# A gated attention and MLP kernel: the last w4 products as fp32r parts at the MLP's end, the second key tile's scores before them, and small weight copies on POOL

## The chip, the cores and the metric

The kernel runs on one core of a Trainium2 chip. A core has five engines with instruction streams of their own: TensorE (PE, matrix products; "PEld" is its weight load), VectorE (DVE), ScalarE (ACT, activations), GpSimd (POOL) and SyncE (SP, which here issues most DMAs). They work on a 128-partition on-chip memory (SBUF) and, for matrix results, on eight PSUM banks of 128 x 512 fp32 elements. Engines wait for each other only by semaphores, and an engine carries out its instructions in the order in which they stand. The metric is device time in microseconds (us). The kernel before takes 912.61 us (median of three runs, 912.49 to 913.4).

## The reference

One input x of 2048 tokens by 448 features goes through two branches. Branch A is attention with 16 query heads of 28 elements that share one key and one value head. Branch B is a shifted token mix and an MLP. A sigmoid gate per token mixes them.

```python
def _A_ref(x, wq, wk, wv, wo):
    q = (x @ wq).reshape(B, S, H, Dh).transpose(0, 2, 1, 3)
    k = x @ wk
    v = x @ wv
    scores = jnp.einsum("bhqd,bkd->bhqk", q, k) * (Dh ** -0.5)
    p = _softmax(scores, axis=-1)
    o = jnp.einsum("bhqk,bkd->bhqd", p, v)
    return o.transpose(0, 2, 1, 3).reshape(B, S, H * Dh) @ wo

def _B_ref(x, w1, w2, w3, w4):
    h = _gelu(_layernorm(x) @ w1)
    ...
    x1 = x + hs
    h2 = _gelu(_layernorm(x1) @ w3) @ w4
    return x1 + h2

g = sigmoid((x * gate_w).sum(-1))
return g * a + (1 - g) * b
```

Here B = 1, S = 2048, D = 448, H = 16, F = 1792 (the width between w3 and w4).

## The kernel before

Three stages follow each other. Stage 1 (to about 125 us) makes queries, keys and values and the token mix, and leaves x1 in SBUF. Stage 2 is the MLP, in four blocks `b` of 512 tokens. Stage 3 is attention, from about 400 us to the end, in 16 units `u`: 512 queries of four heads against all keys.

**Numbers in two parts.** Large products are made with fp32r operands split in a high and a low part (`...h`, `...l`), three products for one: high by high, low by high, high by low. A weight's parts come from `split_w` (w3) and `split_w4` (w4): ACT writes the high part, DVE subtracts to get the low one, and POOL clears a spare corner. The fourth chunk of w3 is only 64 rows deep, so its other 64 rows hold a copy of the raw weight in the low part; `split_w_high` makes it at L114, on ACT.

**The MLP.** In each block `w3_part(b, f)` makes the 14 pieces `f` of 128 hidden features: eleven products into a `mm` bank `g` (L136 to L140), then two activations (`gh` at L688, `gf` at L689) and DVE's difference `gl` (L690). Two pieces later `w4_part` adds the piece's share of w4: for each of four token tiles `t` three 128x448 products into `acc[t]` (L698 to L700). DVE adds `acc` to x1 at L764. While block 0 runs, the weights of pieces to come are split. The last piece of the last block is an exception: it gets one activation in plain fp32 (`gf_late`, L683), its weights come by a DMA of their own (`w4_late`, L740), and its products are left to attention.

**Attention.** A key tile is 128 keys. Its scores (L205) are 12 products of 32 rows each, four heads side by side, into four banks; exponentials (L258) follow on ACT; the products of exponentials and values (`values`, L892) come a round later. A round `c` handles tiles 2c and 2c+1 of the running unit. Eight banks are shared: four `singles` (bank_0 to bank_3), which the MLP knows as its `mm`, `misc` and `mx` banks, and two `pairs` of two banks, which take over the MLP's four `acc` banks. In a full round the first tile's last two heads are copied to SBUF by DVE (L953) so that their pair is free early, and ACT reads that copy last; everything else ACT reads from PSUM. Values results land in two of the singles, DVE adds them into `o` (L813, L817).

**Jobs.** A round can carry a "job" on PE behind its values products: a 128x224 product in column quarters (L843) and one DVE addition. Jobs are the output products of the unit before (eight a unit, from round 12 on) and, in the first rounds, the eight halves of the last w4 piece: three in round 0 (`JOBS_0`), one each in rounds 3, 5, 7, 9 and 11 (`IDLE` and `MAX_AT` leave out the others). Rounds 2 and 10 carry small products for the next unit's maxima (L212) instead; these need its queries, which SP loads (L190) after POOL has cleared `qr` (L783), and which DVE casts (L194).

**The seam.** The order of all instructions is the order of the code. At the end of the MLP stand the scores of key tile 0 (into the singles), then the products of the last but one w4 piece, then round 0.

Of the kernel before, what the change touches and what calls it, by code (L numbers as in the profile page):

```python
# [17 lines left out]
P = 128  # L18
S = 2048
D = 448  # L20
# [22 lines left out]
def gated_mix_kernel(  # L43
# [63 lines left out]
            nc.vector.tensor_tensor(wl[0:64, 3, cols], raw[0:64, 3, cols], f32(wh)[0:64, 3, cols], ALU.subtract)  # L107
            nc.scalar.copy(wl[64:128, 3, cols], raw[64:128, 3, cols])

    def split_w_high(raw, wh, wl):  # L110
        nc.scalar.copy(wh[:, 0:3, :], raw[:, 0:3, :])
        nc.gpsimd.memset(f32(wh)[64:128, 3, :], 0.0)
        nc.scalar.copy(wh[0:64, 3, :], raw[0:64, 3, :])
        nc.scalar.copy(wl[64:128, 3, :], raw[64:128, 3, :])  # L114
# [6 lines left out]
    def split_w(raw, wh, wl):  # L121
        split_w_high(raw, wh, wl)
        split_w_low(raw, wh, wl)

    def split_a(raw, ah, al, c0, c1, high=True):
# [131 lines left out]
    def exps(p, heads, source=None):  # L257
        nc.scalar.activation(p[:, heads], p[:, heads] if source is None else source, AF.Exp, scale=SCALE)  # L258
# [4 lines left out]
    with tc.tile_pool(name="s1b", bufs=1) as s1b, \  # L263
# [325 lines left out]
        kh_of.append(late.tile([P, S], F32R, name="kh"))  # L589
        qh0 = late.tile([P, 512], F32R, name="qh0")  # L590
        ql0 = late.tile([P, 512], F32R, name="ql0")
        gf_late = late.tile([P, 512], F32, name="gf_late")
        w4_late = late.tile([P, D], F32, name="w4_late")
        bigs = ctx.enter_context(tc.tile_pool(name="bigs", bufs=1, side="right", reuse_waits="tile"))
        s2a = ctx2.enter_context(tc.tile_pool(name="s2a", bufs=1, side="right", reuse_waits="tile"))
        w3h, w3l, w4h, w4l = [], [], [], []
# [3 lines left out]
        def big(name):  # L600
            return bigs.tile([P, 2048], F32, tag="big", bufs=2, name=name)
# [10 lines left out]
            nc.sync.dma_start(raw4[i], w4[i * 256:i * 256 + 256, :].rearrange("(c p) n -> p c n", p=P))  # L612

        def split_w3(i):
            split_w(raw3[i], w3h[i], w3l[i])

        def split_w4(i):
            nc.scalar.copy(w4h[i], raw4[i])
# [47 lines left out]
    with tc.tile_pool(name="s2", bufs=1, reuse_waits="tile") as s2, \  # L666
# [11 lines left out]
        def w3_part(b, f):  # L678
            i, k = divmod(f, 2)
            ps = mm_tile(f"g_{b}_{f}")  # L680
            proj(ps, w3h[i][:, :, k * P:(k + 1) * P], w3l[i][:, :, k * P:(k + 1) * P], *acts[b])
            if (b, f) == (NB - 1, NF - 1):
                nc.scalar.activation(gf_late, ps, AF.Gelu_apprx_tanh)  # L683
                return None
            gh = s2.tile([P, 512], F32R, tag="gh", bufs=3, name=f"gh_{b}_{f}")
            gl = s2.tile([P, 512], F32R, tag="gl", bufs=3, name=f"gl_{b}_{f}")
            gf = s2.tile([P, 512], F32, tag="gf", bufs=1, name=f"gf_{b}_{f}")
            nc.scalar.activation(gh, ps, AF.Gelu_apprx_tanh)  # L688
            nc.scalar.activation(gf, ps, AF.Gelu_apprx_tanh)  # L689
            nc.vector.tensor_sub(gl, gf, f32(gh))  # L690
            return gh, gl

        def w4_part(f, t, g, acc, stop=NF - 1):
# [4 lines left out]
            nc.tensor.matmul(ps, gh[:, tok], w4h[i][:, k, :], start=(f == 0), stop=False)  # L698
            nc.tensor.matmul(ps, gh[:, tok], w4l[i][:, k, :], start=False, stop=False)  # L699
            nc.tensor.matmul(ps, gl[:, tok], w4h[i][:, k, :], start=False, stop=(f == stop))  # L700

        for b in range(NB):
            acc = [ps2.tile([P, 512], F32, tag="acc", bufs=4, name=f"acc_{b}_{t}") for t in range(4)]
            gs = {}
            for f in range(NF):
                if f == 9 and b + 1 < NB:
                    mv, rs = layernorm_stats(s2a, b + 1)
                if f == 10 and b + 1 < NB:
                    xt4 = big(f"xt4_{b + 1}")[:, 0:4 * D].rearrange("p (f t j) -> p f t j", f=NE, t=4)
                if f in (10, 11) and b + 1 < NB:  # L710
                    for t in (2 * f - 20, 2 * f - 19):
                        xn = s2a.tile([P, 512], F32, tag="xn", bufs=1, name=f"xn_{b + 1}_{t}")[:, 0:D]
# [12 lines left out]
                if b == 1 and f == 0:  # L725
                    nc.gpsimd.tensor_tensor(gg, invE, gz, ALU.pow)
                    nc.vector.tensor_scalar(gg, gg, 1.0, None, op0=ALU.add)
                    nc.vector.reciprocal(gg, gg)
                    nc.vector.tensor_scalar(gi, gg, -1.0, 1.0, op0=ALU.mult, op1=ALU.add)
                if b == NB - 1 and f == 4:  # L730
                    weigh_x1(0, 4 * b)
                if b == 1 and f == 1:
                    nc.gpsimd.memset(khd, 0.0)
                    for j in range(4):
                        h = slice(32 * j, 32 * j + DH)
                        nc.gpsimd.tensor_copy(khd[h, j * MK:(j + 1) * MK], f32(kh_of[0])[h, 0:MK])
                    qr0 = s2a.tile([P, 512], F32, tag="xn", bufs=1, name="qr_0")
                    nc.gpsimd.memset(qr0, 0.0)
                    q_load(0, qr0)
                    nc.sync.dma_start(w4_late, w4[F - P:F, :])  # L740
                if b == 1 and f == 5:
                    q_high(0, qh0, ql0)
                    q_low(0)
                if f >= 2:
                    for t in range(4):
                        w4_part(f - 2, t, gs[f - 2], acc)
                        if b > 1 and t % 2 == 0 and f < NF - 1:
                            fill()
            if b == NB - 1:
                singles = [mm_tile("bank_0"), mm_tile("bank_1"), misc_tile("bank_2"), max_tile("bank_3")]  # L750
                scores(0, 0, singles)
                nc.scalar.activation(first, powt, AF.Exp)
                p_first = big("p_0_0").rearrange("p (j n) -> p j n", j=4)
                for j in range(4):
                    exps(p_first, slice(j, j + 1), singles[j].unsqueeze(1))
            for t in range(4):
                w4_part(NF - 2, t, gs[NF - 2], acc, NF - 2 if b == NB - 1 else NF - 1)
                if b + 1 < NB:
                    ln_split(b + 1, t, t + 1)
            for t in range(4):  # L760
                if b < NB - 1:
                    w4_part(NF - 1, t, gs[NF - 1], acc)
                xt = x1[:, 4 * b + t, :]
                nc.vector.tensor_add(xt, xt, acc[t][:, 0:D])  # L764
        assert not fills
# [3 lines left out]
    with tc.tile_pool(name="s3", bufs=1, reuse_waits="tile") as s3, \  # L769
# [100 lines left out]

        weigh_x1(NT - 4, NT)

        def w4_products(t, ps, cols):
            by_columns(ps, gf_late, t, w4_late[:, cols])

        def w4_add(t, ps, cols):
            n = NT - 4 + t
            nc.vector.scalar_tensor_tensor(x1[:, n, cols], ps, gi[:, n:n + 1], x1[:, n, cols],
                                           op0=ALU.mult, op1=ALU.add)

        p_of = {0: p_first}

        def score_tiles(u, kt, first, second, third, fourth):
            scores(u, kt, [first, second, third, fourth])
# [9 lines left out]
                if qs.stop == 512:  # L894
                    p_of.pop(k)

        jobs = [(w4_products, w4_add, (t,), cols) for t in range(4) for cols in halves]
        left, right, both, front = slice(0, 1), slice(1, 2), slice(2, 4), slice(0, 2)
        sums, norms, later = [], [], []
        pv = None  # L900
        MAX_AT = 2
# [14 lines left out]
        def run_jobs(ps, n):  # L916
            job_adds(job_products(ps, n))

        NC = NU * NT // 2
        JOBS_0 = (2, 1)  # L920
        IDLE = range(2, 12, 2)
        HINTS = {8 * NT // 2 + 4: [mybir.EngineType.SP],
                 14 * NT // 2 - 2: [mybir.EngineType.DVE, mybir.EngineType.Activation]}
        for c in range(NC):
# [1 line left out]
            k = 2 * c  # L926
            s0, s1, s2, s3_ = singles if c % 2 == 0 else singles[2:] + singles[:2]
            if c == 0:
                pb = score_tiles(u, 1, s2, s3_, s0, s1)
                for j, ps in enumerate((s2, s3_, s0, s1)):  # L930
                    exps(pb, slice(j, j + 1), ps.unsqueeze(1))
                pa = score_tiles(u, 2, *(q[:, h] for q in pairs for h in range(2)))
                nc.vector.tensor_copy(pa[:, front], pairs[0])
                for ps, n in zip((s2, s3_), JOBS_0):
                    run_jobs(ps, n)
                exps(pa, both, pairs[1])
                exps(pa, front)
                pairs.reverse()
                continue
            if c > 1:  # L940
# [43 lines left out]
            elif i == MAX_AT:  # L984
                run_jobs(pairs[0][:, 0], 1)
            values((k - 2, k - 1), s1[:, q0], q1)
            adds = job_products(s0[:, q1], 0 if c in IDLE or c == 1 else 1)
            values_end(v, s1[:, q0], q1)
            job_adds(adds)
            if i == 0 and v < NU - 1:  # L990
# [153 lines left out]
```

## Time and profile before

| what | value |
|---|---|
| median of three runs | 912.61 us (912.49 to 913.4) |
| the profiled execution | 912.95 us |
| its span, from first to last instruction | 911.2 us |
| TensorE clock granted, in tenths, all slices | 9 (9 is 90% or more) |
| ACT busy, 400 to 911 us | 496.67 us of 511 |
| PE busy, 400 to 911 us | 505.70 us of 511 |
| w4 jobs in attention (L843, w_late) | 64 matmul records, 353 ns each |
| w4 products of one piece in the MLP (L698 to L700) | 12 matmuls, about 365 ns each, overlapping |

A row of the timeline reads: start in us, duration, engine, line, operation, output <- inputs, shape, count of instructions merged, and in brackets how long the engine sat idle before and who released it. Matmuls overlap in the array, so the time that one adds is read from start to start. ACT's rows overlap too; what an exponential adds is the distance to the next start. In the page each digit is the busy share of one of 40 slices. A row of the windows gives a stretch of time, its length, and the busy time and instructions of PE, PEld, DVE, ACT and POOL.

### The profile page before, as it was taken

The numbers are of one execution on the slowest core, as the hardware profiler recorded it, in microseconds if no ns is written. First come the engines' busy times: TensorE is split into PE (matmuls) and PEld (weight loads), VectorE is DVE, ScalarE is ACT, GpSimd is POOL, SyncE is SP. The second block draws the span as 40 slices with busy tenths as digits, with TensorE's granted clock in tenths as the row PEclk, the third lists the DMA queues.
The fourth block names the chain that finished last, engine by engine and source line by source line (L and its number), as shares of the span: only waits on it lengthen the run. The fifth ranks groups of instructions, "written<-read, shape, count | busy, mean of one in ns | idle before, by whom it ended". The sixth has DMA issues, their size and how long they took to land.

```text
span 911.2 us, 24150 instructions
## 1 busy us (share of the span) xinstructions
PE 904.7 (99%) x10360; PEld 627.6 (69%) x10360; DVE 517.1 (57%) x961; ACT 633.1 (69%) x1003; POOL 78.3 (9%) x116
## 2 busy tenths in 40 slices
PE   9999999999999999999999999999999999999998
PEld 6788888888888888875555555555555555555554
DVE  4665273631431531136766776776767667767665
ACT  5442344332131231269999999999999999999995
POOL 3243330200000520020000000000000000000000
PEclk9999999999999999999999999999999999999999
DMA  8832654120110020010000001000011000010001
GB/s 306 282 97 54 150 168 131 32 75 1 35 53 2 18 69 1 1 52 24 14 25 14 24 15 55 23 25 17 24 33 36 25 14 25 15 55 13 15 14 44
DMA packets 40582, 47.31 MB, mean 52 GB/s; under 512 B 10136, under 2 KB 28632, under 8 KB 40472
## 3 DMA queue, kind: packets, MB, share of 16 engines
q1 hardware_dynamic: 37304, 40.30, 15.1%
q10 hardware_dynamic: 3168, 5.44, 1.6%
q8 instruction: 82, 1.34, 0.6%
q14 instruction: 28, 0.23, 0.1%
HBM read 32.56 MB, written 11.67 MB: 49 GB/s over the span
## 4 chain that ended last, share of the span: by engine, by line
PE 98%; ACT 2%; DVE 0%; issue 0%
PE bank L892 26%; PE bank L205 19%; PE bank L843 6%; PE acc L700 5%; PE acc L698 5%; PE acc L699 5%; PE g L137 4%; PE g L138 4%; PE g L136 4%; PE pair L205 3%; ACT p L258 2%; PE hs L474 1%; PE hs L475 1%; PE g L139 1%; PE g L140 1%; PE h L137 1%
## 5 line engine op out<-in xcount | busy, mean ns | idle before, releaser
L258 ACT ACTIVATE p<-bank 128x512 f32<-128x512 f32 x514 | 266.1, 605 | 4.7 <-POOL pick L865 1.5
L892 PE MATMUL bank<-p,vext 128*32 128x256 f32 x4064 | 247.7, 382 | 1.0 <-ACT p L258 0.8
L892 PEld LDWEIGHTS bank<-p,vext 128*32 128x32 f32 x4064 | 118.0, 110 | 115.8 <-ACT p L258 53.0
L953 DVE COPY p<-pair 128x1024 f32<-128x1024 f32 x125 | 153.1, 1225 | 57.2 <-PE pair L205 33.0
L688 ACT ACTIVATE gh<-g 128x512 fp32r<-128x512 f32 x55 | 32.9, 598 | 182.8 <-PE g L140 182.8
L817 DVE TENSOR_TENSOR o<-o,bank 128x256 f32<-128x256 f32 x222 | 93.6, 421 | 81.4 <-PE bank L892 70.3
L258 ACT ACTIVATE p<-p 128x1024 f32<-128x1024 f32 x126 | 138.0, 1095 | 0.0
L258 ACT ACTIVATE p<-pair 128x1024 f32<-128x1024 f32 x129 | 136.7, 1060 | 0.0
L690 DVE TENSOR_TENSOR gl<-gf,gh 128x512 fp32r<-128x512 f32 x55 | 38.5, 699 | 165.8 <-ACT gf L689 165.8
L205 PE MATMUL bank<-qh,kh 32*128 32x512 f32 x514 | 115.2, 444 | 0.1
L205 PE MATMUL pair<-qh,kh 32*128 32x512 f32 x510 | 114.1, 444 | 0.0
L205 PE MATMUL bank<-qh,kl 32*128 32x512 f32 x514 | 102.0, 389 | 0.0
L205 PE MATMUL bank<-ql,kh 32*128 32x512 f32 x514 | 101.8, 390 | 0.0
L205 PE MATMUL pair<-qh,kl 32*128 32x512 f32 x510 | 101.1, 389 | 0.0
L205 PE MATMUL pair<-ql,kh 32*128 32x512 f32 x510 | 100.7, 390 | 0.0
L205 PEld LDWEIGHTS bank<-qh,kh 32*128 32x128 f32 x514 | 48.0, 182 | 62.0 <-issue 38.7
L700 PE MATMUL acc<-w4h,gl 128*128 128x448 f32 x220 | 80.7, 367 | 0.0
L698 PE MATMUL acc<-w4h,gh 128*128 128x448 f32 x220 | 80.2, 365 | 0.0
L699 PE MATMUL acc<-w4l,gh 128*128 128x448 f32 x220 | 79.9, 363 | 0.0
L843 PE MATMUL bank<-wof,on 128*32 128x224 f32 (+1 forms) x984 | 69.5, 357 | 0.0
L136 PE MATMUL g<-ah,w3h 128*128 128x512 f32 x168 | 65.5, 390 | 0.0
L137 PE MATMUL g<-al,w3h 128*128 128x512 f32 x168 | 65.4, 390 | 0.0
(207 smaller groups left out, 1397.5 us busy)
## 6 DMA issues: line engine op xcount, KB each, us to landing
qd<-qf ACTq DMA_DIRECT2D x15, 256.0 KB
rb<-rd SPq DMA_DIRECT2D x15, 256.0 KB
x<-in_x_dram SPq DMA_DIRECT2D x4, 896.0 KB
xd<-xt SPq DMA_DIRECT2D x16, 224.0 KB
w34raw<-in_w_dram SPq DMA_DIRECT2D x7, 512.0 KB
qr<-qd SPq DMA_DIRECT2D x64, 56.0 KB
w34raw<-in_w_dram SPq DMA_DIRECT2D x7, 448.0 KB
out_dram<-ot SPq DMA_DIRECT2D x14, 224.0 KB
```

The lines of the kernel that those rows point to most:

```text
L136: nc.tensor.matmul(ps, wh[:, c, :], ah[:, c, :], start=(c == 0), stop=False)
L137: nc.tensor.matmul(ps, wh[:, c, :], al[:, c, :], start=False, stop=False)
L205: nc.tensor.matmul(ps[j], k[h, keys], q[h, :], start=(r == 0), stop=(r == 2), tile_position=(32 * j, 0))
L258: nc.scalar.activation(p[:, heads], p[:, heads] if source is None else source, AF.Exp, scale=SCALE)
L690: nc.vector.tensor_sub(gl, gf, f32(gh))
L698: nc.tensor.matmul(ps, gh[:, tok], w4h[i][:, k, :], start=(f == 0), stop=False)
L699: nc.tensor.matmul(ps, gh[:, tok], w4l[i][:, k, :], start=False, stop=False)
L700: nc.tensor.matmul(ps, gl[:, tok], w4h[i][:, k, :], start=False, stop=(f == stop))
L817: nc.vector.tensor_add(o, o, pv)
L843: nc.tensor.matmul(ps[32 * i:32 * i + 32, :], a[:, c:c + 32], w, start=start, stop=stop, tile_position=(0, 32 * i))
L892: nc.tensor.matmul(pv[32 * j:32 * j + 32, :], vext[:, kt, :], p_of[k][:, j, qs], start=(k == ks[0]), stop=(k == ks[-1]), tile_position=(0, ...
L953: nc.vector.tensor_copy(pa[:, both], pairs[0])
```

## The change

Three edits. First, the last w4 piece of the last block is handled as all others: two activations and a difference make `gh` and `gl`, and twelve fp32r products go into `acc`, before attention starts. `gf_late`, `w4_late`, its DMA and the eight jobs are gone; a tile of the same size (`gap_late`) keeps the memory layout. Second, the scores and exponentials of key tile 1 move from round 0 to the place between the last two pieces' products, and round 0 now handles key tile 2 alone, in bank_0, bank_1 and pair 0. Third, the small copy of w3's fourth chunk goes from ACT to POOL for the seven groups of w3.

```diff
-    def split_w_high(raw, wh, wl):
+    def split_w_high(raw, wh, wl, last=nc.scalar.copy):
         nc.scalar.copy(wh[:, 0:3, :], raw[:, 0:3, :])
         nc.gpsimd.memset(f32(wh)[64:128, 3, :], 0.0)
         nc.scalar.copy(wh[0:64, 3, :], raw[0:64, 3, :])
-        nc.scalar.copy(wl[64:128, 3, :], raw[64:128, 3, :])
+        last(wl[64:128, 3, :], raw[64:128, 3, :])
...
-        gf_late = late.tile([P, 512], F32, name="gf_late")
-        w4_late = late.tile([P, D], F32, name="w4_late")
+        late.tile([P, 512 + D], F32, name="gap_late")
...
-            split_w(raw3[i], w3h[i], w3l[i])
+            split_w(raw3[i], w3h[i], w3l[i], nc.gpsimd.tensor_copy)
...
-            if (b, f) == (NB - 1, NF - 1):
-                nc.scalar.activation(gf_late, ps, AF.Gelu_apprx_tanh)
-                return None
...
+        def first_exps(kt, singles):
+            p = big(f"p_0_{kt}").rearrange("p (j n) -> p j n", j=4)
+            for j in range(4):
+                exps(p, slice(j, j + 1), singles[j].unsqueeze(1))
+            return p
...
-                    nc.sync.dma_start(w4_late, w4[F - P:F, :])
...
-                p_first = big("p_0_0").rearrange("p (j n) -> p j n", j=4)
-                for j in range(4):
-                    exps(p_first, slice(j, j + 1), singles[j].unsqueeze(1))
+                p_first = [first_exps(0, singles)]
             for t in range(4):
-                w4_part(NF - 2, t, gs[NF - 2], acc, NF - 2 if b == NB - 1 else NF - 1)
+                w4_part(NF - 2, t, gs[NF - 2], acc)
...
+            if b == NB - 1:
+                scores(0, 1, singles)
+                p_first.append(first_exps(1, singles))
             for t in range(4):
-                if b < NB - 1:
-                    w4_part(NF - 1, t, gs[NF - 1], acc)
+                w4_part(NF - 1, t, gs[NF - 1], acc)
...
-        jobs = [(w4_products, w4_add, (t,), cols) for t in range(4) for cols in halves]
+        jobs = []
...
             if c == 0:
-                pb = score_tiles(u, 1, s2, s3_, s0, s1)
-                for j, ps in enumerate((s2, s3_, s0, s1)):
-                    exps(pb, slice(j, j + 1), ps.unsqueeze(1))
-                pa = score_tiles(u, 2, *(q[:, h] for q in pairs for h in range(2)))
-                nc.vector.tensor_copy(pa[:, front], pairs[0])
-                for ps, n in zip((s2, s3_), JOBS_0):
-                    run_jobs(ps, n)
-                exps(pa, both, pairs[1])
-                exps(pa, front)
+                pa = score_tiles(u, 2, s0, s1, pairs[0][:, 0], pairs[0][:, 1])
+                exps(pa, left, s0.unsqueeze(1))
+                exps(pa, right, s1.unsqueeze(1))
+                nc.vector.tensor_copy(pa[:, both], pairs[0])
+                exps(pa, both)
                 pairs.reverse()
                 continue
...
-            adds = job_products(s0[:, q1], 0 if c in IDLE or c == 1 else 1)
+            adds = job_products(s0[:, q1], 1)
```

PE at the end of the MLP, where key tile 0's scores are behind it (acc_3_... are the last block's `acc`, gh_3_12 the last but one piece, gh_3_13 the last). Before, the last but one piece's products run straight into key tile 1's scores:

```order
L698 MATMUL acc_3_3_2805<-w4h_6_1517,gh_3_12_3166 128x448
L699 MATMUL acc_3_3_2805<-w4l_6_1518,gh_3_12_3166 128x448
L700 MATMUL acc_3_3_2805<-w4h_6_1517,gl_3_12_3167 128x448
L205 MATMUL bank_2_3211<-qh0_1049,kh_1048 128x512
L205 MATMUL bank_3_3212<-qh0_1049,kh_1048 128x512
L205 MATMUL bank_0_3209<-qh0_1049,kh_1048 128x512
```

Now key tile 1's scores are followed by the last piece's twelve products, of which the first three are shown:

```order
L205 MATMUL bank_0_3212<-qh0_1049,kl_77 128x512
L205 MATMUL bank_1_3213<-qh0_1049,kl_77 128x512
L205 MATMUL bank_2_3214<-qh0_1049,kl_77 128x512
L205 MATMUL bank_3_3215<-qh0_1049,kl_77 128x512
L700 MATMUL acc_3_0_2800<-w4h_6_1516,gh_3_13_3194 128x448
L701 MATMUL acc_3_0_2800<-w4l_6_1517,gh_3_13_3194 128x448
L702 MATMUL acc_3_0_2800<-w4h_6_1516,gl_3_13_3195 128x448
```

The products moved from behind the scores of tile 2 to behind those of tile 1, and onto `acc`.

PE in rounds 0 and 1. Before, key tile 2's scores fill both pairs, w4 jobs follow, and key tile 3's scores use bank_0, bank_1 and pair 0:

```order
L205 MATMUL pair_0_3258<-qh0_1049,kh_1048 128x512 x2
L205 MATMUL pair_1_3259<-qh0_1049,kh_1048 128x512 x2
L205 MATMUL pair_0_3258<-ql0_1050,kh_1048 128x512 x2
L205 MATMUL pair_1_3259<-ql0_1050,kh_1048 128x512 x2
L205 MATMUL pair_0_3258<-qh0_1049,kl_77 128x512 x2
L205 MATMUL pair_1_3259<-qh0_1049,kl_77 128x512 x2
L843 MATMUL bank_2_3211<-w4_late_1052,gf_late_1051 32x224 x8
L843 MATMUL bank_3_3212<-w4_late_1052,gf_late_1051 32x224 x4
L205 MATMUL bank_0_3209<-qh0_1049,kh_1048 128x512
L205 MATMUL bank_1_3210<-qh0_1049,kh_1048 128x512
L205 MATMUL pair_0_3258<-qh0_1049,kh_1048 128x512 x2
```

Now key tile 2's scores use bank_0, bank_1 and pair 0, and key tile 3's, right behind them, the same three:

```order
L205 MATMUL bank_0_3212<-qh0_1049,kh_1048 128x512
L205 MATMUL bank_1_3213<-qh0_1049,kh_1048 128x512
L205 MATMUL pair_0_3290<-qh0_1049,kh_1048 128x512 x2
L205 MATMUL bank_0_3212<-ql0_1050,kh_1048 128x512
L205 MATMUL bank_1_3213<-ql0_1050,kh_1048 128x512
L205 MATMUL pair_0_3290<-ql0_1050,kh_1048 128x512 x2
L205 MATMUL bank_0_3212<-qh0_1049,kl_77 128x512
L205 MATMUL bank_1_3213<-qh0_1049,kl_77 128x512
L205 MATMUL pair_0_3290<-qh0_1049,kl_77 128x512 x2
L205 MATMUL bank_0_3212<-qh0_1049,kh_1048 128x512
L205 MATMUL bank_1_3213<-qh0_1049,kh_1048 128x512
L205 MATMUL pair_0_3290<-qh0_1049,kh_1048 128x512 x2
```

The jobs that stood between the two tiles are gone, and pair 1 is no longer used in round 0.

More of the change, by code (lines that the diff above doesn't have):

```diff
@@ L119, in split_w_low, with split_w @@
         nc.vector.tensor_tensor(wl[0:64, 3, :], raw[0:64, 3, :], f32(wh)[0:64, 3, :], ALU.subtract)
-    def split_w(raw, wh, wl):
-        split_w_high(raw, wh, wl)
+    def split_w(raw, wh, wl, last):
+        split_w_high(raw, wh, wl, last)
         split_w_low(raw, wh, wl)
@@ L691, in w3_part, with w4_part @@
             return gh, gl
-        def w4_part(f, t, g, acc, stop=NF - 1):
+        def first_exps(kt, singles):
[3 more added lines that the diff above has]
+            return p
+        def w4_part(f, t, g, acc):
             i, k = divmod(f, 2)
@@ L699, in w4_part @@
             nc.tensor.matmul(ps, gh[:, tok], w4l[i][:, k, :], start=False, stop=False)
-            nc.tensor.matmul(ps, gl[:, tok], w4h[i][:, k, :], start=False, stop=(f == stop))
+            nc.tensor.matmul(ps, gl[:, tok], w4h[i][:, k, :], start=False, stop=(f == NF - 1))
         for b in range(NB):
@@ L871, in gated_mix_kernel @@
         weigh_x1(NT - 4, NT)
[L873 to L881, printed above, removed]
+        p_of = dict(enumerate(p_first))
         def score_tiles(u, kt, first, second, third, fourth):
@@ L895, in values @@
                     p_of.pop(k)
-        jobs = [(w4_products, w4_add, (t,), cols) for t in range(4) for cols in halves]
-        left, right, both, front = slice(0, 1), slice(1, 2), slice(2, 4), slice(0, 2)
+        jobs = []
+        left, right, both = slice(0, 1), slice(1, 2), slice(2, 4)
         sums, norms, later = [], [], []
```

2 lines of the change are left out of this document (removed).

## The prediction

> **What bounds the kernel now.** I began with the page: busy time, then the chain of work that ended last.
>
> ```profile
> span 911.2 us, 24150 instructions
> PE 904.7 (99%) x10360; PEld 627.6 (69%) x10360; DVE 517.1 (57%) x961; ACT 633.1 (69%) x1003; POOL 78.3 (9%) x116
> PE 98%; ACT 2%; DVE 0%; issue 0%
> ```
>
> TensorE (PE) carries the chain nearly everywhere; the 2% on ScalarE (ACT) is the clue to where it does not. Next the windows: the first two of the four MLP blocks (columns: busy us and instructions of each engine).
>
> ```profile
> 125.80:194.70 68.90, 68.90 (x323) 60.48 (x322) 36.55 (x69) 30.63 (x55) 6.76 (x13) 1.00 0.37 107
> 194.70:263.60 68.90, 68.90 (x323) 60.48 (x322) 23.46 (x45) 17.26 (x32) 1.21 (x2) 1.00 0.12 29
> ```
>
> The first block splits the weights on ACT (30.63 us busy against 17.26), yet PE issues the same 323 matmuls in the same 68.90 us. So ACT is not waited for in the MLP. Then the timeline of ACT in attention. A "round" is two key tiles; its first exponentials come out as one merged row each.
>
> ```profile
> 407.26 2.06 ACT L258 ACTIVATE p<-bank 128x512 f32<-128x512 f32 x4
> 411.17 2.06 ACT L258 ACTIVATE p<-bank 128x512 f32<-128x512 f32 x4
> 415.13 2.07 ACT L258 ACTIVATE p<-bank 128x512 f32<-128x512 f32 x4
> 417.05 1.06 ACT L258 ACTIVATE p<-pair 128x1024 f32<-128x1024 f32 x1
> 417.95 1.09 ACT L258 ACTIVATE p<-p 128x1024 f32<-128x1024 f32 x1
> 418.90 2.10 ACT L258 ACTIVATE p<-bank 128x512 f32<-128x512 f32 x4
> 422.83 0.60 ACT L258 ACTIVATE p<-bank 128x512 f32<-128x512 f32 x1
> 445.93 2.07 ACT L258 ACTIVATE p<-bank 128x512 f32<-128x512 f32 x4
> ```
>
> These are rounds 2, 3, 4 (with its two later exponentials), 5, 6 and 12. Round 4, without a w4 job, takes 418.90-415.13 = 3.77, with ACT's six exponentials end to end: ACT's floor. Rounds 3 and 5, with a job, take 3.96 and 3.93. From round 12 on both programs are the same, so the question is when round 12 begins.
>
> **The change part by part.** Up to 400.3 us almost nothing moves. The last block gains one activation (gf beside gh):
>
> ```profile
> 394.49 0.60 ACT L683 ACTIVATE gf_late<-g 128x512 f32<-128x512 f32 x1 [3.83 <-PE g L140]
> 397.81 2.06 ACT L258 ACTIVATE p<-bank 128x512 f32<-128x512 f32 x4 [1.21 <-PE bank L205]
> 401.38 2.06 ACT L258 ACTIVATE p<-bank 128x512 f32<-128x512 f32 x4 [1.51 <-POOL pick L865]
> ```
>
> It shifts the table load by under 0.60 us, less than the 1.21 us that ACT waits there: nothing; without that cover 0.6. The new subtraction for gl finds VectorE (DVE) idle and is needed 5 us later. Now PE:
>
> ```profile
> 396.81 0.51 PE L205 MATMUL bank<-qh,kh 32*128 32x512 f32 x4
> 397.71 0.47 PE L698 MATMUL acc<-w4h,gh 128*128 128x448 f32 x1
> 400.34 0.51 PE L205 MATMUL bank<-qh,kh 32*128 32x512 f32 x4
> 402.03 1.34 PE L843 MATMUL bank<-w_late,gf_late 128*32 128x224 f32 x24
> 403.30 0.70 PE L205 MATMUL bank<-qh,kh 32*128 32x512 f32 x2
> 404.40 1.93 PE L892 MATMUL bank<-p,vext 128*32 128x256 f32 x32
> 406.26 0.56 PE L205 MATMUL bank<-qh,kh 32*128 32x512 f32 x2
> 407.25 0.50 PE L205 MATMUL pair<-qh,kh 32*128 32x512 f32 x2
> 408.14 1.07 PE L892 MATMUL bank<-p,vext 128*32 128x256 f32 x16
> ```
>
> Before: scores of tiles 1 and 2 from 400.34, three jobs at 402.03 (1.27 us to the next start), scores of tile 3 at 403.30, values of tiles 0 and 1 at 404.40. The jobs fill PE exactly while DVE copies tile 2's bank pair:
>
> ```profile
> 398.63 2.44 DVE L764 TENSOR_TENSOR x<-x,acc 128x448 f32<-128x448 f32 x4 [7.25 <-PE acc L700]
> 402.13 1.23 DVE L933 COPY p<-pair 128x1024 f32<-128x1024 f32 x1 [1.06 <-PE pair L205]
> 406.74 0.85 DVE L194 CAST qh<-qr 128x512 fp32r<-128x512 f32 x1
> 407.51 1.21 DVE L953 COPY p<-pair 128x1024 f32<-128x1024 f32 x1
> 419.86 0.42 DVE L194 CAST qh<-qr 128x512 fp32r<-128x512 f32 x1
> 400.47 0.53 POOL L783 MEMSET qr<- 128x512 f32 x1 [62.90 <-DVE x L764]
> 401.76 5.56 POOL L670 TENSOR_SCALAR x<-x,gi 128x448 f32<-128x448 f32 x4
> ```
>
> After, from these starts:
> - Tile 1's scores still start at 400.34 (their banks are freed at 397.81+2.06 = 399.87), so its exponentials start at 401.38 as before. "Ahead" buys ACT nothing.
> - w4's twelve matmuls follow at +0.90 (397.71-396.81): 401.24. They take 2.63 (400.34-397.71): tile 2's scores start at 403.87. The adds that free pair 0 are two of four that begin 0.92 after the products, so they are done by then.
> - Tile 2's scores are ready at +1.04 (401.38-400.34): 404.91. DVE's copy takes 1.23: 406.14.
> - Tile 3's scores use the **same two banks and the same pair** as tile 2's, and stand next on PE with nothing between: PE waits for the copy, and resumes about 0.05 later (407.25 in the rows follows ACT's release of that pair): 406.2. What queues behind are the values of tiles 0 and 1, whose inputs have long been ready, and all of round 2.
> - Values at +0.89 (408.14-407.25): 407.1, against 404.40. **Loss: 2.7 us.** Tile 4's scores follow at +1.86, its exponentials at +1.00: 409.96 against 407.26, 2.7 again. ACT has been idle meanwhile and cannot hide it.
>
> So three jobs (1.27) leave, 2.63 of products enter, and the 1.3 us that the jobs used to cover is laid bare. Bounds on this term: 2.5 if round 2 gets back the 0.14 between its 3.91 and ACT's floor, 3.0 if each of three hand-overs costs 0.1 more.
>
> **Saved later.** Rounds 3, 5, 7, 9 and 11 lose a job. From round 3 to round 12 before: 445.93-411.17 = 34.76. At ACT's floor, nine times 3.77 = 33.93: **0.83 saved**. DVE's eight w4 adds also vanish, beside work that never holds PE. Bounds: 0.4 if half the job rounds keep their gaps, 2.5 if PE's own pace ruled (a rival, below).
>
> **Moved with it.** The next unit's queries are loaded after a memset on POOL that waits for buffers of the last products; 400.47 follows the products' end by 0.1. That memset becomes about 3.5 later, and the loads behind it on SP's queue, with wo's load ahead of them, too:
>
> ```profile
> 401.02 11.94 SPq L190 DMA_DIRECT2D qr<-qd  x8
> DMA  0000000002094248999999999997510000000000
> ```
>
> That DMA row covers 399 to 408 us in 40 slices: traffic ends by 406, so by 409.5 after. The cast (406.74 before) would come at 409.4 by the 2.7 alone. So 0.1 late; at worst, if the cast had started on the landing, 406.74+3.5 = 410.24 and 0.8 late, and then DVE's copy of tile 4 and the maxima on PE behind it. I take 0.1.
>
> **POOL's copies.** Seven leave ACT:
>
> ```profile
> L114 ACT CAST w3l<-w34raw x7: 403/404/405, 117.6 to 169.9; 64x256 fp32r<-64x256 f32 x7
> 119.75 0.81 POOL L112 MEMSET w3h<- 64x256 f32 x3
> 110.68 0.61 POOL L356 CAST kh<-kl 128x512 fp32r<-128x512 f32 x1
> 125.59 0.39 PE L136 MATMUL g<-ah,w3h 128*128 128x512 f32 x1
> ```
>
> The trace has no POOL copy of 64x256; between 0.27 (a memset of that shape) and 0.61 (a copy of twice the columns). The first runs about 120.0 to 120.6, before the products at 125.59; later ones wait only for their weights, two products ahead of use. Cost and gain: 0, covered by the equal 68.90; without that cover 7 x 0.4 = 2.8 either way. The small w4 load that goes was 200 us from its use: 0.
>
> [...]
>
> **Sum**: +2.7 - 0.83 + 0.1 = about +2.0 us. The profiled span is 911.2, in an execution of 912.95 us; the median of the runs is 912.61, and the sum goes on that: **914.6 us**; a profile of the changed kernel should show a span near 913.2.
>
> **Rivals.**
> 1. The lost time is made up in rounds 3 to 11 at PE's pace, so not slower. PE's own need without a job is
>
> ```profile
> 414.07 0.50 PE L205 MATMUL bank<-qh,kh 32*128 32x512 f32 x2
> 417.64 0.51 PE L205 MATMUL bank<-qh,kh 32*128 32x512 f32 x2
> ```
> 3.57, nine times 32.1, 2.6 less than 34.76: 912.61+2.7-2.6+0.1 = 912.8. It decides if ACT has slack there. Against it: round 4 took 3.77 with no hole on ACT.
> 2. The queries come late enough to hold the maxima: 0.8 more, 915.4. For: the cast follows the landing by under a microsecond now. Against: DVE was busy until then.
> 3. ACT's relief in the first block does reach PE: 912.61+2.0-2.8 = 911.8, faster. Against: 68.90 twice.
> 4. POOL's copies and DVE's subtractions of the same weights hold each other, and so PE: 7 x 0.4 = 2.8 more, 917.4. For: 0.85 against 0.42 for the same cast. Against: in that block DVE works 36.55 of 68.90, and every product has two others between it and its weights.
> That the change does not do what it says is excluded by the order of instructions.
>
> **How the numbers follow.** Forecast 0.65, rival 1 0.10, rival 2 0.13, rival 3 0.07, rival 4 0.05. The forecast's own range, from its bounds (2.5-1.0 to 3.0-0.4+0.3), is 914.1 to 915.5. With the neighbours it becomes 912.8 to 915.9: rival 3, rival 4 and half of rival 1 stay outside, less than 2 in 10. A measurement of this kernel tells about 0.2% (1.8 us) from no change, and the forecast lies just beyond: some three quarters of it count as slower. Slower: 0.49+0.13+0.05 = 0.67. Same: 0.16 and rival 1 but for 0.02 = 0.24. Faster: 0.07+0.02 = 0.09.
>
> **What would show it.** Right: the values of tiles 0 and 1 near 407.1 with a hole on PE of about 1.3 us just before; tile 4's exponentials near 410; rounds 3 to 11 all at 3.77; round 12 about 2 us later than 445.93; the last scores before the final products still at 400.3. Wrong: no hole (the banks were free), rounds below 3.7 (rival 1), the cast of the queries after 410 (rival 2), or a first MLP block other than 68.90 (rivals 3 and 4).

## The result, and the profile after

| | before | changed |
|---|---|---|
| median | 912.66 us | 915.75 us |
| lowest to highest of nine runs each | 912.32 to 914.03 | 915.4 to 917.53 |
| ratio, 95% interval | | 1.0034, 1.0025 to 1.0042 |

The change is slower by 3.1 us. The page of the changed kernel, from an execution of 917.53 us (its span; busy time of each engine; the chain of work that ended last, by engine):

```profile
span 915.7 us, 24056 instructions
PE 906.0 (99%) x10308; PEld 626.5 (68%) x10308; DVE 513.3 (56%) x954; ACT 630.1 (69%) x998; POOL 82.9 (9%) x123
PE 89%; ACT 5%; DMA 4%; DVE 1%; issue 1%; ACTq 0%; DVEq 0%; SPq 0%
```

PE has 52 products fewer and is yet busy 1.3 us longer (0.6 in e1's profile below, 905.3), and ACT's share of the chain has grown from 2% to 5%. The first MLP block is what it was, in a window of 68.90 us:

```profile
125.80:194.70 68.90, 68.90 (x324) 60.43 (x323) 35.71 (x68) 27.43 (x48) 9.76 (x18) 1.00 0.35 103
```

That execution holds a stretch at half clock (0.50 in the windows from 407 to 410 us), told of at the end. So the steps are read from a second profile of the same kernel (first experiment below, 915.69 us, full clock throughout). Its PE, in the timeline (start, duration, instruction; in brackets the idle time before it and what ended it):

```profile
396.59 0.51 PE L205 MATMUL bank<-qh,kh 32*128 32x512 f32 x4
400.12 0.51 PE L205 MATMUL bank<-qh,kh 32*128 32x512 f32 x4
403.64 0.50 PE L205 MATMUL bank<-qh,kh 32*128 32x512 f32 x2
404.43 0.49 PE L205 MATMUL pair<-qh,kh 32*128 32x512 f32 x2 [0.29 <-DVE x L765]
405.86 0.98 PE L205 MATMUL bank<-qh,kh 32*128 32x512 f32 x2 [0.47 <-ACT p L258]
406.71 0.49 PE L205 MATMUL pair<-qh,kh 32*128 32x512 f32 x2
407.60 1.93 PE L885 MATMUL bank<-p,vext 128*32 128x256 f32 x32
409.46 0.50 PE L205 MATMUL bank<-qh,kh 32*128 32x512 f32 x2
```

These are the scores of tiles 0 and 1, tile 2 (its banks, then its pair), tile 3 (the same), the values of tiles 0 and 1, and the scores of tile 4. The same span on DVE and ACT:

```profile
401.93 2.44 DVE L765 TENSOR_TENSOR x<-x,acc 128x448 f32<-128x448 f32 x4 [5.85 <-PE acc L702]
405.43 1.22 DVE L923 COPY p<-pair 128x1024 f32<-128x1024 f32 x1 [1.05 <-PE pair L205]
410.01 0.42 DVE L194 CAST qh<-qr 128x512 fp32r<-128x512 f32 x1
```

```profile
405.21 1.08 ACT L258 ACTIVATE p<-bank 128x512 f32<-128x512 f32 x2 [1.97 <-PE bank L205]
410.47 2.07 ACT L258 ACTIVATE p<-bank 128x512 f32<-128x512 f32 x4 [0.83 <-PE bank L205]
414.25 2.10 ACT L258 ACTIVATE p<-bank 128x512 f32<-128x512 f32 x4
448.38 2.29 ACT L258 ACTIVATE p<-bank 128x512 f32<-128x512 f32 x4
452.49 1.09 ACT L258 ACTIVATE p<-bank 128x512 f32<-128x512 f32 x2
```

PE waits twice. Tile 2's scores have their two banks at 403.64 but their pair only at 404.43, when DVE's four additions (401.93+2.44 = 404.37) are done. Tile 3's wait for the same banks, and for the pair until DVE's copy ends (405.43+1.22 = 406.65). From the end of tile 2's scores (405.39) to tile 3's pair (406.71), 1.3 us, PE makes two products only. ACT has nothing to do for 1.97 us, then for 0.83. The ACT rows are tile 2, then the starts of rounds 2, 3, 12 and 13.

Counted from the start of tile 0's scores (396.81 before, 396.59 here), so that a shift of the whole MLP drops out:

| stretch | forecast | measured, change less before |
|---|---|---|
| to tile 4's exponentials | +2.7 | 13.88 - 10.45 = +3.43 |
| round 2 | +0.1 (queries) | 3.78 - 3.91 = -0.13 |
| rounds 3 to 11 | -0.83 | 34.13 - 34.76 = -0.63 |
| round 12 | 0 | 4.11 - 3.88 = +0.23 |
| round 13 to the end | 0 | 461.41 - 461.39 = +0.02 |
| sum | +2.0 | +2.92 |

Less 0.22 for the earlier start this is the 2.7 between the spans, 913.9 and 911.2. The medians lie 3.1 apart, since the profiled execution of the kernel before was 0.3 above its median (912.95 against 912.66). Round 13 began before the change at:

```profile
449.81 0.60 ACT L258 ACTIVATE p<-bank 128x512 f32<-128x512 f32 x1
```

### The profile page after: what moved, and what is told of

It reads as the page before. It is cut to its first block, busy times and chain, and to the rows that moved or that the text cites. A ratio compares the mean times of both kernels' runs of the same rounds, so it can differ in the third digit from the quotient of the medians.

```text
span 915.7 us, 24056 instructions
## 1 busy us (share of the span) xinstructions
PE 906.0 (99%) x10308; PEld 626.5 (68%) x10308; DVE 513.3 (56%) x954; ACT 630.1 (69%) x998; POOL 82.9 (9%) x123
## 4 chain that ended last, share of the span: by engine, by line
PE 89%; ACT 5%; DMA 4%; DVE 1%; issue 1%; ACTq 0%; DVEq 0%; SPq 0%
PE bank L885 24%; PE bank L205 18%; PE bank L844 5%; PE acc L702 5%; PE acc L700 5%; PE acc L701 5%; PE g L136 4%; PE g L138 4%; PE g L137 4%; ACT p L258 4%; PE pair L205 3%; DMA qd<-qf 2%; PE g L139 1%; PE g L140 1%; PE hs L474 1%; PE hs L475 1%
## 5 line engine op out<-in xcount | busy, mean ns | idle before, releaser
L258 ACT ACTIVATE p<-bank 128x512 f32<-128x512 f32 x516 | 268.9, 618 | 8.1 <-PE bank L205 5.6
```

## The experiments

Each time is a median beside runs of the kernel before on the same chip (912.36 for e1 to e4, 912.69 for e5 to e8, 912.6 for e9 to e11). Where the text says "start", it counts from tile 0's scores as above.

**e1, the change again**, unedited.

> The changed kernel once more, for a profile that may show the full TensorE clock. Theory (hole and clock): the order of the work costs about 2.4 us against the kernel before, and in some executions the granted clock falls to about 0.66 for 5 us behind PE's wait in round 1, for about 1.5 us more; so executions near 915.4 and others near 917, and in a profile at full clock tile 4's exponentials start near 410.6 (412.07 in the first profile). Rival (order alone): the clock has no part, every profile shows tile 4 near 412 and the executions spread evenly.

Measured: 915.71, ratio 1.004 (1.0026 to 1.0054). The loss is there without the low clock; its profile is the one read above, with tile 4's exponentials at 410.47. No execution of e1 shows the low clock (a mean of 1.0 in all five), so that part of the expectation is not tested here; one takes 916.8 at full clock.

**e2, tile 2 on other banks.** Tile 2 takes the two banks and the pair that tile 3 does not use:

```diff
-                pa = score_tiles(u, 2, s0, s1, pairs[0][:, 0], pairs[0][:, 1])
-                exps(pa, left, s0.unsqueeze(1))
-                exps(pa, right, s1.unsqueeze(1))
-                nc.vector.tensor_copy(pa[:, both], pairs[0])
+                pa = score_tiles(u, 2, s2, s3_, pairs[1][:, 0], pairs[1][:, 1])
+                exps(pa, left, s2.unsqueeze(1))
+                exps(pa, right, s3_.unsqueeze(1))
+                nc.vector.tensor_copy(pa[:, both], pairs[1])
```

> The changed kernel with tile 2 on bank_2, bank_3 and pair 1, so that tile 3 needs none of its banks. Theory (shared banks make the hole): tile 3's scores start at about 405.4 and not 406.85, no low clock follows, the values of tiles 0 and 1 come near 406.4 instead of 408.4; ACT then has tile 2's last part ahead of tile 3 and tile 4 starts near 409.8; 914.4 to 914.9 us, every execution. Rival (ACT is simply out of work there, whatever the banks): tile 4 still near 410.6 or later and the time of the changed kernel.

Measured: 914.71, ratio 1.0022 (1.0013 to 1.0032). PE in e2, tiles 2 and 3 and the values:

```profile
403.70 0.50 PE L205 MATMUL bank<-qh,kh 32*128 32x512 f32 x2
403.87 0.50 PE L205 MATMUL pair<-qh,kh 32*128 32x512 f32 x2
...
404.49 0.40 PE L205 MATMUL bank<-qh,kh 32*128 32x512 f32 x2
...
405.46 1.93 PE L885 MATMUL bank<-p,vext 128*32 128x256 f32 x32
407.73 0.99 PE L205 MATMUL bank<-qh,kh 32*128 32x512 f32 x2 [0.33 <-ACT p L258]
```

Both waits are gone: this pair is written 0.17 after the banks, tile 3 follows at 404.49, and the values start 1.76 after tile 2's scores instead of 3.96. That is 2.2 us, yet the time falls by 1.0 only. A part stops at tile 4's scores (0.33, for ACT, which makes tile 2's late exponential ahead of tile 3's), so that tile 4's exponentials gain 1.50: they come 12.38 after the start (409.01-396.63) instead of 13.88. e7 takes that away. Another 0.83 is lost in round 2, which takes 4.61 (413.62-409.01) instead of 3.78, while DVE's cast of the queries idles 1.96 us for their load; e7 and e9 return to that.

**e3, the wait filled.** Ten products of zeros into a bank that is free then, between the scores of tiles 2 and 3:

```diff
                 pa = score_tiles(u, 2, s0, s1, pairs[0][:, 0], pairs[0][:, 1])
+                for _ in range(10):
+                    nc.tensor.matmul(s2[:, 0:256], warm[:, 0:P], warm, start=True, stop=True)
```

> The changed kernel with ten small products of zeros (128x256, bf16) into bank_2, whose result nobody reads, between the scores of tile 2 and those of tile 3; they only occupy PE while it waits. Theory (the low clock follows from PE's idle time): no execution with a low clock, all near 915.4 and none near 917; tile 4 at 410.6. Rival (the clock falls for another reason, or the wait is not where the time goes): the same spread as the changed kernel. If the filler lengthens the path instead, all executions are later by up to 1.1 us.

Measured: 915.8, ratio 1.0037 (1.0023 to 1.0051).

```profile
403.18 0.49 PE L205 MATMUL bank<-qh,kh 32*128 32x512 f32 x2
...
404.86 1.26 PE L922 MATMUL bank<-warm 128*128 128x256 bf16 x10
...
407.15 1.93 PE L885 MATMUL bank<-p,vext 128*32 128x256 f32 x32
```

1.26 us of added work moves nothing: the values start 3.97 after tile 2's scores, 3.96 without it. So PE is really idle there, held by the banks. Whether the filler also prevents the low clock stays open, since e1 beside it had none to prevent.

**e4, POOL's copies alone**: the kernel before with this part of the change only (as in the diff above):

```diff
-            split_w(raw3[i], w3h[i], w3l[i])
+            split_w(raw3[i], w3h[i], w3l[i], nc.gpsimd.tensor_copy)
```

> The kernel before with the third edit alone: the seven small copies of w3 on POOL. Theory: nothing, 912.6 within 0.3 us, first MLP block 68.90 us. Rival A (ACT's relief reaches PE): up to 2.8 us faster. Rival B (POOL and DVE hold each other over the weights): up to 2.8 us slower.

Measured: 912.48, ratio 1.0002 (0.9993 to 1.0011). The first MLP block and the copies, in a window and in the groups by line:

```profile
125.80:194.70 68.90, 68.90 (x324) 60.44 (x323) 34.52 (x65) 27.04 (x48) 9.64 (x18) 1.00 0.36 105
```
```profile
L114 POOL CAST w3l<-w34raw 64x256 fp32r<-64x256 f32 x7 | 3.6, 520 | 22.9 <-DMA w34raw<-in_w_dram 22.8
```

PE issues without a pause in all 68.90 us, with ACT 3.6 us less busy than before (30.63). A copy takes 520 ns on average, inside the 0.27 to 0.61 that bounded it, but single ones do not all. In the first profile of the changed kernel, which has the same seven copies, four take 0.39 to 0.40, and three that lie beside a subtraction on DVE take 0.67 to 0.76 (at 127.99, 132.91 and 139.44). DVE's three subtractions beside the second of these take 1.30 together (at 132.57), against 1.10 for the same three in the kernel before. One of the four short copies (0.39, at 169.36) has subtractions beside it too, so what lengthens the others is not shown. PE does not wait for it: this part is neutral.

**e5, without the five later jobs**: the kernel before with

```diff
-        jobs = [(w4_products, w4_add, (t,), cols) for t in range(4) for cols in halves]
+        jobs = [(w4_products, w4_add, (t,), cols) for t in range(4) for cols in halves][:3]
```

> The kernel before without the five w4 jobs of rounds 3 to 11 (it leaves out five of the eight halves of the last w4 piece of the last block). Theory: these jobs cost 0.83 us, since ACT's floor of 3.77 us sets rounds 3 to 11 without them: 911.8 us, round 12 at 445.1. Rival (PE's pace sets these rounds): 2.6 us faster, 910.0.

Measured: 914.26, ratio 1.0017 (1.0008 to 1.0026): slower by 1.6 with work taken out, where 0.8 less was expected. From round 3's start to round 13's it took 38.22, against 38.64 before and 38.24 in e1, and the last output left earlier than before, at 906.28 against 907.18. What is longer lies behind it. The last DMA issue and the instruction queue in the last 6 us, of the kernel before and then of e5 (start, duration, queue; packets, MB, share):

```profile
907.18 0.86 ACTq L1041 DMA_DIRECT2D out_dram<-ot  x2
...
q14 instruction: 3, 0.02, 1.2%
```
```profile
906.28 0.85 ACTq L1041 DMA_DIRECT2D out_dram<-ot  x2
...
q14 instruction: 4, 0.03, 1.6%
```

The span ends 4.0 us after that issue before (911.2), 5.8 after it in e5 (912.1). One more packet of instructions comes in, and in the DMA row of those 6 us it stands alone, at about 911.8, some 3 us behind all other traffic. e11 tests this.

**e6, tile 2 on four single banks, tile 3 on both pairs**, as tiles 1 and 2 stood before the change:

```diff
-                pa = score_tiles(u, 2, s0, s1, pairs[0][:, 0], pairs[0][:, 1])
...
+                pa = score_tiles(u, 2, s2, s3_, s0, s1)
+                for j, ps in enumerate((s2, s3_, s0, s1)):
+                    exps(pa, slice(j, j + 1), ps.unsqueeze(1))
...
+            if c == 1:
+                pb = score_tiles(u, 3, *(q[:, h] for q in pairs for h in range(2)))
+                nc.vector.tensor_copy(pb[:, 0:2], pairs[0])
+                exps(pb, both, pairs[1])
+                exps(pb, slice(0, 2))
```

> The changed kernel with tile 2 on the four singles and tile 3 on the two pairs. Theory (the hole comes from shared banks, and 0.7 us of it from the wait for the fourth addition to x before a pair may be written): tile 2's exponentials start at 404.85 instead of 405.35 and go through, PE has no hole above 0.5 us, no low clock; tile 4 near 409.0; 913.5 to 914.0 us. Rival (ACT's empty time from 403.3 to 404.8 sets it all): 914.5 or more.

Measured: 914.1, ratio 1.0017 (1.0008 to 1.0026), a little above what was expected. Its profile is of an execution of 916.16, so only distances within it are read, beside e7.

**e7, banks and order**: e2, and tile 2's copied half is exponentiated after tile 3:

```diff
-                exps(pa, both)
...
-            if 1 < c < NC - 1:
+            if 0 < c < NC - 1:
                 exps(pa, both)
```

> As the kernel with tile 2 on bank_2, bank_3 and pair 1, and tile 2's last two heads (the copy in SBUF) exponentiated after tile 3 instead of before it. Theory: ACT need not wait for the copy; tile 4 near 409.2, so 0.5 us less than without this, 913.8 to 914.3. Rival (PE sets it): the same time as without it.

Measured: 914.6, ratio 1.0021 (1.0012 to 1.003). The 0.5 less than e2 (914.71) that was expected is not there. In e6 and in e7 tile 4's exponentials come 11.8 after the start, against 13.88 in the change: 2.06 gained, and 0.56 more than in e2. But round 2 then takes 5.22 and 4.86 instead of 3.78, and more than half of the gain is gone again. Round 3's start in e7 (round 2 starts at 408.02), and round 2 on DVE and PE:

```profile
412.88 2.07 ACT L258 ACTIVATE p<-bank 128x512 f32<-128x512 f32 x4 [0.90 <-PE pair L205]
```
```profile
409.18 0.43 DVE L194 CAST qh<-qr 128x512 fp32r<-128x512 f32 x1 [1.67 <-DMA qr<-qd]
```
```profile
408.71 1.07 PE L885 MATMUL bank<-p,vext 128*32 128x256 f32 x16 [0.16 <-ACT p L258]
410.79 0.30 PE L212 MATMUL pair<-khd,qh 128*32 128x64 bf16 x16 [1.01 <-DVE p L939]
410.90 1.05 PE L885 MATMUL bank<-p,vext 128*32 128x256 f32 x16
```

DVE idles 1.67 us until the queries land. Its copy of tile 4's pair stands behind the cast, the maxima (L212) wait for that copy, and the second half of the values stands behind them: 2.2 after the first instead of 1.0 (411.12 and 412.12 in e1). That points to the load, and e9 and e10 take it up.

**e8, the five later jobs cut in ten**: the kernel before, 112 columns in each of rounds 2 to 11 instead of 224 in every other:

```diff
+        jobs = [(w4_products, w4_add, (t,), cols) for t in range(4) for cols in halves][:3]
+        jobs += [(w4_products, w4_add, (h // 2,), slice(D // 2 * (h % 2) + o, D // 2 * (h % 2) + o + D // 4))
+                 for h in range(3, 8) for o in (0, D // 4)]
...
-            adds = job_products(s0[:, q1], 0 if c in IDLE or c == 1 else 1)
+            adds = job_products(s0[:, q1], 0 if c == 1 else 1)
```

> The kernel before with the five later w4 jobs cut into ten of 112 columns, one in each of rounds 2 to 11. Theory (PE has about 0.2 us to spare in a round without a job, a half of a job costs about 0.25): 0.3 to 0.6 us faster than before, 912.0 to 912.3. Rival (a small product costs nearly as much as a larger one): every round at 3.9, up to 0.5 us slower.

Measured: 913.09, ratio 1.0004 (0.9995 to 1.0013); no gain. The values of rounds 4, 7 and 8, and round 7's job:

```profile
415.82 1.93 PE L892 MATMUL bank<-p,vext 128*32 128x256 f32 x32
...
427.26 1.93 PE L892 MATMUL bank<-p,vext 128*32 128x256 f32 x32
...
429.28 0.40 PE L843 MATMUL bank<-w_late,gf_late 128*32 128x112 f32 x8
...
431.34 1.93 PE L892 MATMUL bank<-p,vext 128*32 128x256 f32 x32
```

A quarter job fits in at 3.81 a round (three rounds in 427.26-415.82), which is also the pace without a job (below). Round 7 takes 4.08: its job starts 2.02 after the values where those of the rounds around it start at 1.75. It waits there for DVE's addition into `o`; why that was late was not followed. Round 2, which holds a job beside the maxima, takes 4.12 instead of 3.91. These two take the gain back.

**e9, banks, order and queries**: e7, with the load of wo behind the query loads on SP's queue:

```diff
-        nc.sync.dma_start(wof, wo.rearrange("(g p) n -> p g n", p=P))
...
         q_fetch(1)
+        nc.sync.dma_start(wof, wo.rearrange("(g p) n -> p g n", p=P))
```

> As banks_and_order (tile 2 on the other two banks and pair, its last exponential after tile 3's), and the load of wo now stands behind the four loads of the next unit's queries on SyncE's queue. Nothing is left out. Theory 'the late queries are the bound once the hole is gone': the loads are issued near 400.9 instead of 403.6, the cast of the queries no longer shows an idle time that ends with a DMA and starts near 408 instead of 409.18, the second half of the values follows the first by 1.0 instead of 2.2, tile 4 to round 3 takes 3.8 instead of 4.86, and the time is 1.1 less than that of banks_and_order: 913.5. What is then left against the kernel before is work on TensorE, 2.63 of products for 1.27 of jobs, less 0.4 saved later. Rival 'round 2 is long for another reason' (the exponentials moved behind tile 3's): the loads come earlier, the round stays at 4.6 or more, 914.6.

Measured: 913.67, ratio 1.0012 (1.0003 to 1.0021). SP's queue, DVE and ACT in e9:

```profile
400.46 2.56 SPq L190 DMA_DIRECT2D qr<-qd  x4
```
```profile
407.49 0.65 DVE L194 CAST qh<-qr 128x512 fp32r<-128x512 f32 x1
```
```profile
408.08 2.10 ACT L258 ACTIVATE p<-bank 128x512 f32<-128x512 f32 x4
...
411.83 2.16 ACT L258 ACTIVATE p<-bank 128x512 f32<-128x512 f32 x4
```

The cast waits for nothing, and round 2 takes 3.75. Against e7 the time is 0.9 less. Tile 4's exponentials come 11.83 after the start, 1.38 later than before the change (10.45): about the 1.36 by which 2.63 of products exceed 1.27 of jobs. On PE it is 1.24: tile 4's scores start 10.69 after the start (406.94) against 9.45 before (406.26), with no idle time in the rows between tile 2's scores and them. So little or nothing is left of the waits that the change made.

**e10, the queries ahead, in the change as it is**: the same move of one line in the changed kernel.

> The change with the load of wo behind the four query loads on SyncE's queue, nothing else. Theory 'in the change the hole hides the late queries': loads issued near 400.9 instead of 404, but tile 3 waits for tile 2's banks as before, tile 4 to round 3 takes 3.8 as it did, and the time stays at 915.7. Rival 'the late loads cost the change time too': 0.8 to 1.1 less, 914.7.

Measured: 915.53, ratio 1.0034 (1.0021 to 1.0046). The loads are issued at 400.56, and round 3 still starts 17.66 after the start, as in e1 (414.25-396.59). So the late load costs the change nothing that shows: the wait for the banks hides it.

**e11, four jobs**: e5 with `[:4]` in place of `[:3]`.

> The kernel before with four of the eight halves of the last w4 piece: one of the five later ones stays, four are left out. Theory 'without_later_jobs was slow only at its very end, where one more packet of the instruction queue came in about 911 us, 3 us after the last others': with a program of another length that packet does not come, the span ends 4.0 after the last output is issued instead of 5.8, and the time is 912.4 to 912.5 (0.2 to 0.3 under the kernel before, since job-free rounds save 0.16 each and later rounds give part of it back). Rival 'fewer jobs cost time elsewhere or the end is long for another reason': 914.2 again.

Measured: 912.05, ratio 0.9996 (0.9987 to 1.0005), 0.3 below what was expected. The last issue, and the instruction queue in the last 6 us:

```profile
906.15 0.85 ACTq L1041 DMA_DIRECT2D out_dram<-ot  x2
...
q14 instruction: 3, 0.02, 1.3%
```

No packet comes late, and the span (910.2) ends 4.05 after the issue. One job more and the program is 2.2 us faster than e5 (1.9 between the two profiled spans), of which 1.8 lie in that end. e5's time says nothing on jobs; its rounds do.

## Why the prediction was right, and where it was not

The forecast was 914.6 with 914.1 to 915.5 as its own range; 915.75 lies 0.25 beyond that and inside the whole range. That it is still inside is luck: the range reached so far up only for rival 2, whose mechanism did not act. The direction and the mechanism are the forecast's; two terms were mis-sized, both in the direction of too small a loss.

- **The hole on PE: right, and shown.** The step "tile 3's scores use the same two banks and the same pair as tile 2's" holds in e1's rows; other banks (e2) take away 2.2 at the values, and filling the hole (e3) costs nothing.
- **Its size: 0.7 too small.** The step that failed is "the adds that free pair 0 are two of four, so they are done by then". The pair waits for the last of the four, which ends at 404.37: it is written 0.79 after the banks in e1, 0.17 after in e2, where tile 2 takes the other pair. There it need not wait for the last, which ends at 404.43. This difference of 0.62 is most of the 0.73 between 2.7 and 3.43, since the copy and all behind it move with it.
- **"At ACT's floor, 3.77": too much saved.** The 3.77 of round 4 before was read between two rounds with a job. The lasting pace shows at the values on PE. Rounds 3 and 11 before, and rounds 3, 4, 11 and 12 of e1:

```profile
411.82 1.94 PE L892 MATMUL bank<-p,vext 128*32 128x256 f32 x32
...
442.69 1.94 PE L892 MATMUL bank<-p,vext 128*32 128x256 f32 x32
```
```profile
414.93 1.93 PE L885 MATMUL bank<-p,vext 128*32 128x256 f32 x32
...
418.74 1.93 PE L885 MATMUL bank<-p,vext 128*32 128x256 f32 x32 [0.27 <-ACT p L258]
...
445.44 1.93 PE L885 MATMUL bank<-p,vext 128*32 128x256 f32 x32 [0.15 <-ACT p L258]
...
449.25 1.93 PE L885 MATMUL bank<-p,vext 128*32 128x256 f32 x32 [0.28 <-ACT p L258]
```

  Eight rounds take 30.87 before, 3.86 each, and 30.51 in e1, 3.81 each. So a job cost the two rounds that share it 0.1, not 0.2. Before, PE waits 0.26 to 0.28 for ACT only in every other of these rounds, and not in the round behind a job; in e1 it waits so in nearly all. ACT's starts look 3.76 apart at first and fall back to 3.8 and 3.9 in rounds 8 to 10. What sets 3.81 and not 3.77 was not followed.
- **"From round 12 on both programs are the same": not in time.** Round 12 has its output job in both, but takes 4.11 instead of 3.88, as its values now wait 0.28 first. Saved in all: 0.40, the low bound of the prediction's term. e5 and e9 give 0.42 and 0.33 over the same rounds.
- **The queries: no cost, for another reason.** The memset on POOL did not move (400.25 in e1, 400.47 before). What moved is wo's load, issued at 403.55 instead of 400.44, with the query loads behind it on the queue. The term was 0.1; round 2 even gained 0.13. The cast starts at 410.01, later than the 410 that was to speak for rival 2, but right behind DVE's copy of the values (409.67+0.42), not behind its load. Rival 2 ("queries late enough to hold the maxima") is false of the change (e10), but true of it without the hole: 0.9 us between e7 and e9.
- **POOL's copies, the table load, the MLP: 0, as said.** e4 for the copies, 68.90 for the first block, and in e1 tile 1's scores 3.53 after tile 0's, as before. Rivals 3 and 4 fall with that. Rival 4's 7 x 0.4, a wait for a whole copy at each of seven, no run shows: in the changed kernel three copies took 0.67 to 0.76 against 0.39 to 0.40 of the others, one group of subtractions 1.30 against 1.10 before, and PE waited for none of it (68.90 there and in e4). The cast of 0.85 that was to speak for rival 4 ran while POOL weighed x (401.76+5.56), those of 0.42 behind that work, at 419.86 before and at 410.01 in e1; it is no subtraction of a weight. Rival 1 (the lost time made up at PE's own pace, 3.57 a round) falls by 3.81.

So the 2.9 of the table are about 2.05 of waiting for banks (13.88 against 11.83 in e9, where ACT's order and the load differ too) and 1.36 by which the new products exceed the three jobs of round 0, less 0.5 that come back in rounds 2 to 12. No version with the new products was as fast as the kernel before; the best, e9, is 1.1 slower.

## What to carry to other kernels

A move of work ahead of a pipeline can cost more than the work, as here, where the next two users of a PSUM bank became neighbours: look up for each tile which banks it takes, who frees them last, and what stood between. A wait that is removed can uncover the next: here the banks hid a late load, and mending the banks alone gained 1.0 to 1.1 (e2, e7), the load alone nothing that can be told (0.2), both 2.0. A round's pace is read over several rounds at the engine whose end counts, not from one round that may be spending slack.

## What the runs showed of the hardware

**The clock was at half behind a short wait, in one profile.** The changed kernel's first profile, in windows of 1 us (busy us and instructions of PE, PEld, DVE, ACT, POOL; granted clock; DMA share; GB/s), and PE there:

```profile
406.00:407.00 1.00, 1.00 (x6) 0.51 (x6) 0.80 (x1) 0.61 (x2) 1.00 (x2) 0.82 1.01 380
407.00:408.00 1.00, 1.00 (x11) 0.69 (x10) 0.00 (x0) 0.89 (x1) 1.00 (x1) 0.50 1.03 394
...
410.00:411.00 1.00, 1.00 (x20) 0.36 (x12) 0.42 (x1) 0.12 (x1) 0.00 (x0) 0.97 0.00 0
```
```profile
408.43 2.71 PE L885 MATMUL bank<-p,vext 128*32 128x256 f32 x32
```

By the means of these windows the clock was at half for 0.36+3.00+0.06 = 3.4 us, right behind the hole, and the values took 2.71 instead of 1.93. Over the span that lowers the mean clock by 0.002. Tile 4's exponentials came at 412.07, 1.45 later from the start than in e1. Of 20 executions of the three kernels that keep the hole (the change, e1, e10) three show a mean clock of 0.998 and take 916.9 to 917.5; of 32 of the three without it (e2, e7, e9) none does. But e5, which has no such hole, shows 0.998 in two of 11, at 913.93 and 914.43 and so no later than its others. That the hole causes the half clock fits the first counts, which are small, and was not shown. Here PE had idled 0.29 and 0.47 us, the same two waits as in e1's rows, where the clock stays full, and it was busy while the clock was low. In e5's profile the clock falls at the end, where PE has no more work: none from 907 on, with a mean clock of 1.00 in 907 to 909, 0.82 in 909 to 910 and 0.50 in 910 to 912.

**One end of a program was 1.8 us longer than the others.** In e5 one packet of the instruction queue came in about 3 us behind the last other traffic, and the span ended 5.8 after the last issue; in the eleven other profiles whose end was read it ended 3.9 to 4.1 after it, and in the ten of these whose queue was read there was one packet fewer in the last 6 us. The programs differ little in length, e5 and e11 by one job. That the longer end comes from this packet, and which engine it was for, is not shown.
